# A hand-ordered kernel with one load queue, three row tiles loaded ahead of the first weights, and norms on GpSimd

## The chip, the core and the metric

The kernel runs on one core of one Trainium2 chip. A core has five engines that run on their own: TensorE (PE in the profile, with PEld for its weight loads), VectorE (DVE), ScalarE (ACT), GpSimd (POOL) and SyncE (SP), which here only issues transfers. DMAs are issued from SP's queue (q1 in the profile) and from ACT's queue (q10). The metric is the time of one execution in microseconds of device time, smaller is better; the median of three runs is given for the kernel before.

## What is computed

Two branches share one normalised input and are multiplied at the end:

```python
x  = A_q                                    # 1 x 2048 x 512, bfloat16
xn = layernorm(x)
# branch A: shift convolution, long convolution along the sequence, gate
k_shift = sum over t<4 of shift(A_k, 3 - t) * A_shift_k[:, 3 - t]
kv = k_shift * A_v
y  = irfft(rfft(pad(kv)) * rfft(pad(A_ssm_k)))[:2048]   # length 4096
s  = xn * (y + kv * A_ssm_D)
# branch B: gated feed-forward
h  = gelu(xn @ B_w_gate) * (xn @ B_w_up)    # 512 -> 1792
g  = silu(h @ B_w_down)                     # 1792 -> 512
out = x + s * g
```

The Fourier transforms are done as matrix products with tables of sines that the kernel builds itself.

## The kernel before

**Stages.** The 2048 rows are 16 row tiles of 128, in four quarters of four. The rows are taken so that partition p holds rows 16p to 16p+15. For each quarter, `ln` takes mean and variance of each row tile (`bn_stats`, `bn_aggr`, lines 875 and 876), the reciprocal root (for quarter 0 a square root on ACT, line 888, and a reciprocal on DVE, line 889; for the others a power on POOL, line 892), and writes the normalised tile XN (line 901 on ACT, line 902 on DVE or POOL). `xn_transpose` makes xnT, the transposed tile that PE needs: for quarter 0 four PE transposes per row tile (line 925) and evacuations from PSUM (the accumulator memory, 8 banks) by ACT or DVE; for the later quarters one transposing DMA on SP (line 914). `unit` multiplies one quarter's xnT with 128 columns of the gate and up weights (a product of four matrix products each, line 1200, recorded under the helper's line 649), takes the gelu on ACT (line 1220) and multiplies on DVE into HT (1226 and 1229). For the first two column groups of quarter 0 the work comes in sixteen half products, one row tile each, so that PE can begin before all four tiles are there. `down` multiplies HT with the down weights, in groups of 4, 5 and 5 column groups.

**The long convolution.** The filter A_ssm_k is loaded as four tiles h0 to h3 (Hn), transposed on DVE in 32 x 32 blocks (line 944, tasks 50 to 53, one per tile, about 2 us each), goes through a first transform on PE (`stage1` "H", line 984, eight tasks: 97, 92, 102, 117, 112, 107, 122, 87), is evacuated by ACT, stored to the scratch ZH through ACT's queue (tasks 91 to 126), read back (BH) and transformed again (line 1055, `psf`). The key side: `kshift` forms the four-tap shift convolution of a group of four row tiles on DVE (lines 1032 to 1038, about 1.2 us per instruction, eight per group) and the product with V (line 1040, giving KV0 to KV3, tasks 138, 146, 154, 162). `stage1` "K" (line 973) transforms KV on PE (u = 6 and 7, tasks 236, 237, 241, 242, read KV3), stores to ZK through SP, reads back (BK), transforms again (`psk`), multiplies spectra on DVE, transforms back (`inverse`, `psi`), stores to ZI and reads back (BI) for the last transform (line 1304).

**What sets the order.** Every instruction belongs to one of 802 numbered tasks. SEQ, a list written out in the program, gives the order in which tasks are emitted; a "b" behind a number takes the task's second engine. Each engine runs its own tasks in that order. `Trk` adds the semaphore waits from what tasks read and write, PSUM banks among them. `Sched.run` walks SEQ and gives each task a planned start and end from its costs; these plan times decide nothing at run time, except that a task which needs a bank or a buffer gets the one that is free first by the plan (`Pool_.find`). LAND holds the planned landing of each load; FIRST the time from which an engine is free in the plan; TAKEN a delay, per store that ACT issues early (`eng == "ACT"`), of the loads still under way.

**Loads.** ORDER gives the order in which loads are issued: x00, x01, x02 are row tiles 0, 1 and 2 with 3 (128, 128 and 256 KB); w0 to w3 are column groups of the gate and up weights (w0 two groups of 256 KB, the others 512 KB each); h0 to h3 the filter; k, v, d the keys, values and down weights. All are issued on SP, except w0, whose two loads are issued on ACT:

```python
"w": lambda i: load_w(i, ("ACT", "ACT") if i == 0 else ("SP", "SP"))
```

PE begins with 12 products without meaning (`warm_up`), which raise its clock before the first real product.

Of the kernel before, what the change touches and what calls it, by code (L numbers as in the profile page):

```python
# [22 lines left out]
LN_EPS = 1e-5  # L23
TURN = 8192
N_WARM = 12
ORDER = "x00 x01 w0 x02 w1 h0 h1 w2 h2 h3 D0 x1 s0 k0 w3 k1 d0 k2 d1 v0 v1 k3 v2 v3 x2 x3"
SEQ = (
# [23 lines left out]
)  # L51
NF_BANKS = 8
ISSUE = 470.0
LAND = {"x0_0": 3000, "x0_1": 4850, "wg0": 4500, "wu0": 6300, "x0_2": 6650, "wg1": 8150, "wu1": 9650, "h0": 11200, "h1": 12500, "wg2": 14000, "wu2": 15500, "h2": 16800, "h3": 18050, "D": 18500, "kz": 12600, "x1": 19350, "sk": 21850, "kh1": 23200, "kh113": 23400, "k0": 24700, "wg3": 26200, "wu3": 27700, "k1": 29000, "wd0": 31500, "k2": 32900, "wd1": 37000, "v0": 39000, "v1": 40400, "k3": 41700, "v2": 42950, "v3": 44250}
W_XT, W_SW, W_BK, W_BH, W_ZI, W_BI, W_ZK, W_MI, W_G1 = 850000, 690000, 685000, 688000, 310000, 575000, 600000, 329000, 150000
T_BH, T_BK, T_BI, T_X = 900.0, 500.0, 1500.0, 900.0
NC_PAIRS = 4
# [238 lines left out]
class Sched:  # L296
# [6 lines left out]
    OVL = {"DVE": 80.0, "ACT": 100.0}  # L303
    DMA_BW = 370.0
    SHARE_BW = 300.0
    FIRST = {"loads": 300.0, "SP": 37000.0, "ACT": 1600.0}
    DRAIN, DRAIN2 = 121.0, 97.0
    EARLY, LATE, SHARED, WAIT, TAKEN = 31000.0, 36500.0, 47000.0, 3300.0, 0.0

    def __init__(self):  # L310
        self.tasks = []
# [40 lines left out]
    def run(self):  # L352
        free = dict(self.FIRST)
        pipe = 0.0
# [66 lines left out]
def build_kernel(nc, A_q, A_k, A_v, A_shift_k, A_ssm_k, A_ssm_D, B_w_gate, B_w_up, B_w_down, out):  # L421
    with ExitStack() as es0:
# [104 lines left out]
        def dsem(name):  # L527
            return DSem(nc.alloc_semaphore(name), name)
# [92 lines left out]
        def dma(eng, out_ap, in_ap, sem, r, w):  # L621
            trk.dma(eng, lambda e: e.dma_start(out=out_ap, in_=in_ap), sem, r=r, w=w)  # L622
# [3 lines left out]
        def load(name, out_ap, in_ap, w_res, w_buf, nbytes, ring="SP", r=(), rb=()):  # L626
            sem = dsem("d_" + name)
            last_load[0] = S.add([("loads", ISSUE)], lambda e: dma(ring, out_ap, in_ap, sem, r, w_res), r=rb, w=w_buf, nbytes=nbytes, land=float(LAND[name]))

# [194 lines left out]
        def load_x0(t):  # L824
            ts = slice(*((0, 1), (1, 2), (2, 4))[t])
            load(f"x0_{t}", X[:, ts, :], x_dr[:, ts, :], R_X[ts], bX[0][ts], 131072 * (ts.stop - ts.start))

        def load_w(i, rings=("SP", "SP")):
            f0, n = FC[i]
            for nm, W, src, ring in (("g", Wg, wg_dr, rings[0]), ("u", Wu, wu_dr, rings[1])):  # L830
                load(f"w{nm}{i}", W[:, :, 128 * f0:128 * (f0 + n)], src[:, :, 128 * f0:128 * (f0 + n)], [R_Wc[nm, i]], [bW[nm][i]], 131072 * n, ring)

        def load_h(k, ring):
            load(f"h{k}", Hn[:, k, :], h_dr[:, k, :], [R_Hn[k]], [bHn[k]], 524288, ring)
# [27 lines left out]

        for what in ORDER.split():
            if what[0] == "x" and len(what) == 3:
                load_x0(int(what[2]))
                continue
            {"k": load_k, "v": load_v, "w": lambda i: load_w(i, ("ACT", "ACT") if i == 0 else ("SP", "SP")), "x": load_x, "d": load_wd, "h": lambda i: load_h(i, "SP"), "s": load_taps, "D": load_d}[what[0]](int(what[1:]))


        t_stats = [None] * NT  # L870
# [457 lines left out]
        for j in range(6):  # L1328
            d_out.append(dsem(f"d_out{j}"))
            g = G[:, 2 * j:2 * j + 2, :].rearrange("p t d -> p (t d)")  # L1330
            x = X[:, 2 * j:2 * j + 2, :].rearrange("p t d -> p (t d)")
# [17 lines left out]
def bass_recurrent_scan__ssm_conv_h3__glu_gated_geglu__prompt_kernel(  # L1349
    nc: bass.Bass,  # L1350
    A_q: bass.AP,
    A_k: bass.AP,
    A_v: bass.AP,
    A_shift_k: bass.AP,
    A_ssm_k: bass.AP,
    A_ssm_D: bass.AP,
    B_x: bass.AP,
    B_w_gate: bass.AP,
    B_w_up: bass.AP,
    B_w_down: bass.AP,  # L1360
    out: bass.AP,
):
    build_kernel(nc, A_q, A_k, A_v, A_shift_k, A_ssm_k, A_ssm_D, B_w_gate, B_w_up, B_w_down, out)
# [28 lines left out]
```

## Time and profile before

| | us |
|---|---|
| median of 3 runs (lowest, highest) | 186.76 (186.75, 187.11) |
| profiled execution, whole | 186.69 |
| its span, first to last instruction | 184.9 |
| PE busy / share of the span | 178.2 / 96% |
| DVE busy | 168.3 / 91% |
| ACT busy | 141.7 / 77% |
| POOL busy | 17.7 / 10% |
| mean granted clock of PE | 0.999 |

Times within the trace count from the first instruction of the span. A row of the timeline has start, length, engine (a q marks an issue by the engine's sequencer), line, operation, what it writes `<-` reads, shape, the number of instructions merged, and in brackets the idle time before it and what ended it. Matrix products overlap in PE, so that the length of one row reaches into the next: the pace is read from start to start. A row of waits has the total, the number of times, and the longest. A row of grouped instructions has busy time and mean ns, then the idle time before them. A DMA row ends with the median from issue to landing.

### The profile page before, as it was taken

How to read it: one execution, taken by the hardware profiler on the slowest of the kernel's cores; microseconds unless marked ns; L12 is line 12 of the kernel's file. 1: busy time of each engine (PE TensorE's matmuls, PEld its weight loads, DVE VectorE, ACT ScalarE, POOL GpSimd, SP SyncE). 2: the span in 40 equal slices, each digit the busy share in tenths (PEclk: the TensorE clock that was granted, in tenths of full speed). 3: DMA queues.
4: the chain of work that ended last, by engine and by line, in shares of the span. 5: the costliest groups of instructions: out<-in, count | busy, mean ns of one | idle time of the engine just before them, and what ended most of it. 6: DMA issues, size and time to landing. Idle time of an engine off the chain costs nothing.

```text
span 184.9 us, 3811 instructions
## 1 busy us (share of the span) xinstructions
PE 178.2 (96%) x1522; PEld 77.7 (42%) x1522; DVE 168.3 (91%) x250; ACT 141.7 (77%) x204; POOL 17.7 (10%) x29
## 2 busy tenths in 40 slices
PE   8599999979999999999999999999999999999993
PEld 3474444434443443433434433343333344445552
DVE  5998999999999999999579999999999997459994
ACT  3599798996489999998379798887898875238771
POOL 4000190890000000002200000000000000000000
PEclk9999999999999999999999999999999999999999
DMA  5999999999891959887999999688317154599338
GB/s 150 340 376 397 307 362 375 397 415 249 244 303 62 292 212 273 258 286 273 214 311 263 309 377 346 222 312 261 113 60 273 34 184 136 179 381 395 127 119 281
DMA packets 38683, 48.38 MB, mean 262 GB/s; under 512 B 9483, under 2 KB 28427, under 8 KB 38666
## 3 DMA queue, kind: packets, MB, share of 16 engines
q1 hardware_dynamic: 31082, 39.23, 67.7%
q10 hardware_dynamic: 7584, 8.91, 13.9%
q8 instruction: 12, 0.20, 0.4%
q14 instruction: 5, 0.04, 0.1%
HBM read 27.39 MB, written 14.68 MB: 228 GB/s over the span
## 4 chain that ended last, share of the span: by engine, by line
PE 85%; DMA 6%; DVE 4%; SPq 3%; issue 0%; ACT 0%
PE psall L649 67%; DMA Hn<-in_A_ssm_k_dram 6%; PE psall L1250 6%; PE psall L1055 6%; SPq L622 3%; PE psall L973 2%; DVE HTr L944 2%; PE psall L984 2%; PE psall L1304 2%; DVE HT L1226 0%; DVE HT L1229 0%; DVE G L1272 0%; DVE G L1271 0%; ACT G L1269 0%; DVE NB__68 L897 0%
## 5 line engine op out<-in xcount | busy, mean ns | idle before, releaser
L649 PE MATMUL psall<-xnT,Wg 128*128 128x512 bf16 (+1 forms) x248 | 55.6, 359 | 0.0
L649 PE MATMUL psall<-xnT,Wu 128*128 128x512 bf16 (+1 forms) x248 | 54.9, 359 | 0.1
L649 PE MATMUL psall<-Wd,HT 128*128 128x512 bf16 (+1 forms) x182 | 40.3, 368 | 1.0 <-DVE HT L1229 1.0
L1220 ACT ACTIVATE GE<-psall 128x512 bf16<-128x512 f32 x54 | 31.8, 608 | 9.4 <-PE psall L649 6.8
L649 PEld LDWEIGHTS psall<-xnT,Wu 128*128 128x128 bf16 x248 | 22.1, 98 | 26.3 <-issue 2.0
L649 PEld LDWEIGHTS psall<-xnT,Wg 128*128 128x128 bf16 x248 | 21.6, 98 | 26.5 <-issue 2.6
L1229 DVE TENSOR_TENSOR HT<-psall,GE 128x512 bf16<-128x512 f32 x36 | 24.1, 683 | 6.0 <-PE psall L649 5.8
L640 ACT ACTIVATE BO<-psall 128x1024 bf16<-128x1024 f32 x21 | 21.1, 1024 | 6.3 <-PE psall L1055 3.9
L649 PEld LDWEIGHTS psall<-Wd,HT 128*128 128x128 bf16 x182 | 16.2, 98 | 21.5 <-issue 2.6
L1158 DVE TENSOR_TENSOR HSW<-KB,HSW 128x2048 bf16<-128x2048 bf16 x16 | 19.1, 1218 | 0.1
L640 ACT ACTIVATE HSW<-psall 128x1024 bf16<-128x1024 f32 x14 | 13.9, 1023 | 5.4 <-PE psall L1055 5.3
L1038 DVE TENSOR_TENSOR KAC<-KAC,KTM 128x2048 bf16<-128x2048 bf16 x12 | 15.2, 1263 | 0.1
L1036 DVE TENSOR_TENSOR KTM<-KK,SKB 128x2048 bf16<-128x2048 bf16 x12 | 14.8, 1234 | 0.0
L640 ACT ACTIVATE KB<-psall 128x1024 bf16<-128x1024 f32 x14 | 13.8, 1029 | 1.3 <-PE psall L1055 1.2
L1250 PE MATMUL psall<-Wd,HT 128*64 128x512 bf16 (+1 forms) x112 | 12.7, 366 | 0.0
L1261 ACT ACTIVATE G<-psall 128x512 bf16<-128x512 f32 x12 | 6.9, 595 | 7.2 <-PE psall L649 7.1
L875 DVE BATCH_NORM_STATS2 stats<-X 128x6 f32<-128x512 bf16 x16 | 10.7, 682 | 1.1 <-DMA X<-in_A_q_dram 1.1
L640 ACT ACTIVATE U__73<-psall 128x512 bf16<-128x512 f32 x18 | 10.8, 637 | 0.1
L640 ACT ACTIVATE XN<-psall 128x1024 bf16<-128x1024 f32 x10 | 10.0, 1030 | 0.4 <-DMA ZH<-XN 0.4
L1263 DVE SCALAR_TENSOR_TENSOR G<-G,psall 128x512 bf16<-128x512 bf16 x12 | 7.9, 679 | 2.4 <-ACT G L1261 2.3
L1181 DVE TENSOR_TENSOR HSW<-HSW 128x2048 bf16<-128x2048 bf16 x8 | 9.6, 1216 | 0.0
L1158 DVE TENSOR_TENSOR KB<-KB,HSW 128x2048 bf16<-128x2048 bf16 x8 | 9.6, 1218 | 0.0
(94 smaller groups left out, 182.6 us busy)
## 6 DMA issues: line engine op xcount, KB each, us to landing
BH<-ZH SPq DMA_DIRECT2D x8, 512.0 KB, 5.4
HSW<-HSW SPq DMA_DIRECT2D x16, 256.0 KB, 2.9
BK<-ZK SPq DMA_DIRECT2D x8, 512.0 KB, 5.8
ZI<-BO ACTq DMA_DIRECT2D x16, 256.0 KB, 2.3
BI<-ZI SPq DMA_DIRECT2D x8, 512.0 KB, 6.7
ZH<-XN ACTq DMA_DIRECT2D x5, 512.0 KB, 3.4
ZK<-AST SPq DMA_DIRECT2D x5, 512.0 KB, 2.8
Hn<-in_A_ssm_k_dram SPq DMA_DIRECT2D x4, 512.0 KB, 9.2
```

Source lines behind the costliest of these rows:

```text
L640: return h.activation(o, i, ACTF.Copy, scale=scale)
L649: return h.matmul(o, lhsT=l, rhs=r, start=st, stop=sp)
L875: t_stats[t] = op([("DVE", 670.0)], lambda e, h, t=t: h.bn_stats(stats[:, t, :], X[:, t, :]), r=[bX[q][t % 4]], w=[bst[t]], rr=[R_X[t]], w ...
L1036: op([("DVE", dur)], lambda e, h, j=j, m=m: h.tensor_tensor(KTM[:, m.slot, :, :], kk(j), sk(j), ALU.mult), r=need + [bSKB[j], a], w=[m], r ...
L1038: op([("DVE", dur)], lambda e, h, m=m: h.tensor_tensor(KAC[:, a.slot, :, :], KAC[:, a.slot, :, :], KTM[:, m.slot, :, :], ALU.add), r=[m], ...
L1055: trk.op("PE", lambda h: h.matmul(ps(s, i)[b, :], lhsT=wt(col)[a, :], rhs=data(col)[a, :], start=n < 16, stop=n >= len(todo) - 16, tile_po ...
L1158: return hd.tensor_tensor(pair(KB, *(2 * DM * z for z in slots())) if to else x, k, x, ALU.mult)
L1181: return hd.tensor_tensor(x, x, y, ALU.add)
L1220: gelu_set.append(op([("ACT", act(512))], lambda e, h: h.activation(GE[:, g.slot, :], bank(pg), ACTF.Gelu_apprx_tanh), r=[pg], w=[g], rr=l ...
L1229: op([("DVE", dve(512, 1))], lambda e, h: h.tensor_tensor(HT[:, q % 2, m, :], bank(pu), GE[:, g.slot, :], ALU.mult), r=[pu, g], w=[bHT[q][m]],
L1250: trk.op("PE", lambda h, m=m, i=i, c=c: h.matmul(pc()[c, :], lhsT=HT[:, q % 2, m, 128 * jt + 64 * i:128 * jt + 64 * i + 64], rhs=Wd[:, m, ...
L1263: op([("DVE", dve(512, 1))], lambda e, h, g=g, pc=pc: h.scalar_tensor_tensor(out=g, in0=g, scalar=1.0, in1=pc(), op0=ALU.add, op1=ALU.mult ...
```

## The change

Four things change in the text. The two loads of w0 are issued on SP like the rest, and ORDER puts x02 ahead of w0. LAND gets new values. The plan's TAKEN becomes 1450 and ACT is free at 800 in place of 1600. SEQ is a new order of the same 802 tasks, with another choice of engine for nineteen of them. The choice of POOL for the norms of quarter 0 was there before (line 903) and is now taken for row tiles 0 to 2.

```diff
-ORDER = "x00 x01 w0 x02 w1 h0 h1 w2 h2 h3 D0 x1 s0 k0 w3 k1 d0 k2 d1 v0 v1 k3 v2 v3 x2 x3"
+ORDER = "x00 x01 x02 w0 w1 h0 h1 w2 h2 h3 D0 x1 s0 k0 w3 k1 d0 k2 d1 v0 v1 k3 v2 v3 x2 x3"
 SEQ = (
-    "0 17 18 ... 47 2 9 3 4 10 6 8 7 5 55 56 63 1 11 57 64 58 66 "
-    "65 67 77 127 78 68 79 59 80 352 81 364 350 60 61 69 362 70 82 62 71 72 73 365 75 74 353 83 363 84b 366 351 354 85 86b 367 12 370 358 368 359 "
+    "0 17 18 ... 47 2 9 4 55 5 56 3 57 8 63 64 65b 58 66 1 6 67 "
+    "59 77 78b 79 68b 60 80 61 69 70 71b 10 127 62 362 350 81 82 72 364 73 352 351 365 83 353 363 74 85 84b 368 358 356 86b 75 354 357 369 370 "
...
-LAND = {"x0_0": 3000, "x0_1": 4850, "wg0": 4500, "wu0": 6300, "x0_2": 6650, "wg1": 8150, ... "wd0": 31500, "k2": 32900, "wd1": 37000, "v0": 39000, ... "v3": 44250}
+LAND = {"x0_0": 3100, "x0_1": 3560, "wg0": 6050, "wu0": 6850, "x0_2": 5060, "wg1": 8550, ... "wd0": 31300, "k2": 32600, "wd1": 34900, "v0": 36200, ... "v3": 41400}
...
-    FIRST = {"loads": 300.0, "SP": 37000.0, "ACT": 1600.0}
+    FIRST = {"loads": 300.0, "SP": 37000.0, "ACT": 800.0}
...
-    EARLY, LATE, SHARED, WAIT, TAKEN = 31000.0, 36500.0, 47000.0, 3300.0, 0.0
+    EARLY, LATE, SHARED, WAIT, TAKEN = 31000.0, 36500.0, 47000.0, 3300.0, 1450.0
...
-            ... "w": lambda i: load_w(i, ("ACT", "ACT") if i == 0 else ("SP", "SP")), ...
+            ... "w": lambda i: load_w(i), ...
```

The order that this gives to each engine, at the places that matter below (numbers are tasks, names are what they write):

| engine | before | after |
|---|---|---|
| DVE, start | 9, 10, 6, 7 (tables), 55 and 56 (statistics and aggregate of tile 0), 11, 57, 64 (reciprocal 0), 58, 65 (norm 0), 67, 68 (norm 1), 59, 60, 61, 70, 62, 71 (norm 2), 73, 74 (norm 3), 84, 86 (evacuations), 367, 355, 50, 51 (HTr0, HTr1), 373, 385, 389, 52, 53 (HTr2, HTr3), 361 | 9, 55, 56, 57, 64, 58, 6, 67, 59, 78 (evacuation), 60, 61, 70, 10, 62, 73, 74 (norm 3), 84, 86, 11, 355, 7, 367, 373, 50, 51, 389, 385, 361, 52, 53 |
| POOL, start | 2, 3, 4, 5 (tables, constants) | 2, 4, 5, 3, then 65, 68, 71 (norms 0, 1, 2) |
| POOL, from 22 us | 127, 15, 129, 14, 130, 128 (tap copies and table products), 455 (power), 16, 54 (the fold of D into HTr, line 951), 76 | 127, 15, 128, 130, 54 (fold), 129, 14, 455, 16, 76 |
| PE, start | two transposed tiles, half products, with the other two transposes among them; 14 half products before the first full unit, 11 full units before task 97 | the same, all 16 half products before the first full unit, 12 full units before task 97 |
| DVE, near 37 us | ... 416, 135, 456, 412, 421, 425 (last HT of quarter 0) | ... 421, 105, 416, 456, 412, 425, 135 |
| DVE, last tasks up to 162 (KV3) | among them 650, 651 (statistics of tile 15) | 646 (statistics of tile 13); 650, 651 behind 162 |
| PE, near 80 us | 532, 172, 236, 533, 534, 241, 237, 242 | the same |
| ACT, near 27 us | 101 (store of ZH2) behind 94; 96 behind 415 | 96 and 101 behind 419 |
| ACT, near 84 us | 243, 244 (K evacuations), 657 (XN14), 168, 535 (tanh) | 243, 535, 244, 655 (XN12), 168 |
| DVE, near 84 us | 652 (variance), 552, 556, 239, 557, 654 (bias), 655, 656, 658 (norms) | 652, 239, 654, 656, 657, 658 |

The nineteen tasks with another engine: norms 65, 68, 71 from DVE to POOL; evacuations 78, 178, 198, 275 and 739 and norms 564 and 657 from ACT to DVE; 169, 179, 274, 294, 301, 346, 733 and norms 565 and 655 from DVE to ACT.

More of the change, by code (lines that the diff above doesn't have):

```diff
@@ L53 @@
 ISSUE = 470.0
-LAND = {"x0_0": 3000, "x0_1": 4850, "wg0": 4500, "wu0": 6300, "x0_2": 6650, "wg1": 8150, "wu1": 9650, "h0": 11200, "h1": 12500, "wg2": 14000, "wu2": 15500, "h2": 16800, "h3": 18050, "D": 18500, "kz": 12600, "x1": 19350, "sk": 21850, "kh1": 23200, "kh113": 23400, "k0": 24700, "wg3": 26200, "wu3": 27700, "k1": 29000, "wd0": 31500, "k2": 32900, "wd1": 37000, "v0": 39000, "v1": 40400, "k3": 41700, "v2": 42950, "v3": 44250}
+LAND = {"x0_0": 3100, "x0_1": 3560, "wg0": 6050, "wu0": 6850, "x0_2": 5060, "wg1": 8550, "wu1": 10030, "h0": 11330, "h1": 12600, "wg2": 14100, "wu2": 15600, "h2": 16900, "h3": 18150, "D": 18600, "kz": 12600, "x1": 19500, "sk": 21850, "kh1": 23200, "kh113": 23400, "k0": 24700, "wg3": 26200, "wu3": 27700, "k1": 29000, "wd0": 31300, "k2": 32600, "wd1": 34900, "v0": 36200, "v1": 37500, "k3": 38800, "v2": 40100, "v3": 41400}
 W_XT, W_SW, W_BK, W_BH, W_ZI, W_BI, W_ZK, W_MI, W_G1 = 850000, 690000, 685000, 688000, 310000, 575000, 600000, 329000, 150000
@@ L866, in build_kernel @@
                 continue
-            {"k": load_k, "v": load_v, "w": lambda i: load_w(i, ("ACT", "ACT") if i == 0 else ("SP", "SP")), "x": load_x, "d": load_wd, "h": lambda i: load_h(i, "SP"), "s": load_taps, "D": load_d}[what[0]](int(what[1:]))
+            {"k": load_k, "v": load_v, "w": lambda i: load_w(i), "x": load_x, "d": load_wd, "h": lambda i: load_h(i, "SP"), "s": load_taps, "D": load_d}[what[0]](int(what[1:]))
         t_stats = [None] * NT
```

44 rows, old and new, of the table SEQ are left out of this document.

## The prediction

> **What bounds the kernel now.** I read the page's busy shares first, then what PE waited for, then busy time by stretch, then the timeline of DVE where PE was not full. The sum below is made against the profiled execution: 186.69 us, of which 184.9 are span and 1.79 lie around it; the median of the three runs is 186.76, 0.07 more.
>
> ```profile
> PE 178.2 (96%) x1522; PEld 77.7 (42%) x1522; DVE 168.3 (91%) x250; ACT 141.7 (77%) x204; POOL 17.7 (10%) x29
> PE psall L925 <- DVE XN L902: 1.7, 2, 1.5
> PE psall L649 <- DVE HT L1229: 1.0, 1, 1.0
> PE psall L984 <- DVE HTr L944: 0.2, 1, 0.2
> 8.68:21.80 13.12, 12.95 (x100) 7.36 (x101) 11.99 (x16) 11.60 (x24) 0.00 (x0) 1.00 1.06 368
> 17.70:80.20 62.50, 61.34 (x411) 26.09 (x408) 62.40 (x82) 54.28 (x82) 13.57 (x13) 1.00 0.95 292
> 80.00:155.00 75.00, 75.00 (x803) 29.59 (x802) 70.22 (x95) 60.05 (x77) 2.05 (x2) 1.00 0.75 234
> 155.00:181.20 26.20, 26.20 (x229) 12.96 (x198) 20.29 (x34) 14.63 (x20) 0.00 (x0) 1.00 0.66 234
> ```
>
> In the stretches the columns after the length are PE, PEld, DVE, ACT, POOL, granted clock, DMA. PE is full from 8.68 to 181.20 but for 0.2 us near 21.7 and about 1 us near 38; at 1.00 of its clock there is no other slack to win. What can be won is the front (products before 8.68 are thin) and those two waits. The second reading matters more: DVE is busy 62.40 of the 62.50 us from 17.70 to 80.20. Where DVE starts and where it ends:
>
> ```profile
> 5.84 11.83 DMA Hn<-in_A_ssm_k_dram
> 17.70 3.96 DVE L944 STREAM_TRANSPOSE HTr<-Hn 128x1024 int32<-128x1024 int32 x2 [0.61 <-DMA Hn<-in_A_ssm_k_dram]
> 78.96 1.21 DVE L1040 TENSOR_TENSOR V<-KAC,V 128x2048 bf16<-128x2048 bf16 x1
> 80.45 0.39 PE L973 MATMUL psall<-V,FT 64*128 64x512 bf16 x2
> ```
>
> The third long-filter load (h2) lands at 5.84 + 11.83 = 17.67, DVE begins its transpose at 17.70 and never rests until the last shifted product KV3 (task 162) ends at 78.96 + 1.21 = 80.17. PE's task 236 needs KV3 and starts at 80.45. So PE may come at most 0.28 us earlier there unless DVE does. Before 80 us the kernel has two bounds within 0.3 us of each other, and a change that speeds PE alone is stopped at task 236.
>
> **The change, part by part.**
>
> *First weights from ACT's queue to SP's.* Two issues leave ACT (which delayed its table load) and stand behind the three X loads on SP.
>
> ```profile
> X<-in_A_q_dram SPq DMA_DIRECT2D x2, 128.0 KB, 3.6
> Wg<-in_B_w_gate_dram ACTq DMA_DIRECT2D x1, 256.0 KB, 4.0
> Wu<-in_B_w_up_dram ACTq DMA_DIRECT2D x1, 256.0 KB, 4.9
> 3.99 0.69 DVE L875 BATCH_NORM_STATS2 stats<-X 128x6 f32<-128x512 bf16 x1 [1.10 <-DMA X<-in_A_q_dram]
> 5.84 4.03 SPq L622 DMA_DIRECT2D Hn<-in_A_ssm_k_dram  x2
> out_dram<-G SPq DMA_DIRECT2D x3, 128.0 KB, 2.2
> ```
>
> The X loads are issued first on SP now too, so their issue does not move; they only stop sharing the DMA engines. The first row tile is in use at 3.99; bounds for its landing L: 3.97 (nothing won) and 0.7 + 2.2 = 2.9 (the quickest 128 KB transfer here). I take 3.6. Later loads are issued about 1 us later on SP, but SP already sits in one issue for microseconds (h2 and h3 take 4.03 for two), so their order of bytes, not their issue, sets the landing: the same bytes stand ahead of h2, and I leave 17.67 as it is, plus or minus 0.2.
>
> *Norms of row tiles 0 to 2 to GpSimd, evacuation 78 from ACT to DVE.* POOL has no such row. Bounds from its rows of the same width:
>
> ```profile
> 22.54 0.64 POOL L1013 COPY SKB<-SKR 128x512 bf16<-128x512 bf16 x1 [19.79 <-DMA SKR<-in_A_shift_k_dram]
> 23.15 1.24 POOL L755 TENSOR_TENSOR TM<-TAB 128x512 f32<-128x512 f32 x1
> 5.19 0.69 DVE L875 BATCH_NORM_STATS2 stats<-X 128x6 f32<-128x512 bf16 x1
> 5.79 0.14 DVE L889 RECIPROCAL mv<-mv 128x1 f32<-128x1 f32 x1
> 6.01 0.38 DVE L902 TENSOR_SCALAR XN<-X,mv 128x512 bf16<-128x512 bf16 x1
> 6.45 0.40 PE L925 MATMUL psall<-ident,XN 128*128 128x128 bf16 x4 [1.45 <-DVE XN L902]
> 11.30 1.25 PE L649 MATMUL psall<-xnT,Wg 128*128 128x128 bf16 x8
> 18.88 1.89 PE L649 MATMUL psall<-xnT,Wu 128*128 128x512 bf16 x8
> 20.61 1.03 PE L649 MATMUL psall<-xnT,Wg 128*128 128x512 bf16 x4
> ```
>
> One norm costs 0.64 to 1.24 there against 0.38 on DVE; I take 0.8, nearer the copy, as it also has one tensor input. The first norm starts at about L + 1.65 (statistics, their aggregate, the second tile's statistics, reciprocal, at the spacing of the rows above: 0.73 + 0.10 + 0.60 + 0.22), so its transpose can start at 3.6 + 1.65 + 0.8 + 0.05 = 6.1 in place of 6.45, the second 0.8 later. On DVE the second tile's small steps and task 6 reach to L + 2.2, then come statistics (0.6), evacuation 78 (0.4 with its wait), an aggregate (0.1) and the fourth statistics (0.6): the third reciprocal near L + 3.9, the third norm on POOL until L + 4.9, the fourth on DVE until L + 5.5. The third tile is transposed and evacuated near L + 5.95; eight half products of a quarter unit each (0.22, from the unit below) and 0.2 of waiting for the fourth end the front at L + 7.95 = 11.55. Now the x8 row at 11.30 begins with four short ones (0.22), so the first full unit starts at 11.52 with two half products (0.45) still owed: 11.97. Won: 0.4 us, with bounds +1.0 (L 2.9, norm 0.64) and -1.4 (L 3.97, each norm 1.24 plus a hold-up of 0.45).
>
> *That hold-up,* seen where POOL and DVE both read two tensors:
>
> ```profile
> 31.73 1.21 DVE L1038 TENSOR_TENSOR KAC<-KAC,KTM 128x2048 bf16<-128x2048 bf16 x1
> 35.27 1.68 DVE L1038 TENSOR_TENSOR KAC<-KAC,KTM 128x2048 bf16<-128x2048 bf16 x1
> 35.84 1.41 POOL L951 TENSOR_TENSOR HTr<-HTr,Dt 128x128 bf16<-128x128 bf16 x1
> ```
>
> The same addition takes 1.21 alone and 1.68 beside POOL's fold. The Trainium skill, "SBUF — State Buffer", section "Who interferes with whom", says that a DVE instruction with two SBUF inputs or in a two-port mode and a GpSimd instruction share a port pair, and that the later one blocks for the whole instruction. That speaks against the norms on GpSimd; the 0.47 us row agrees in kind. By the page the fourth norm and the phase product (task 6) on DVE would each block POOL or be blocked once; by the rows alone I charge nothing in the middle value and 0.45 a norm at the bad end.
>
> *New order, PE.* PE now does twelve full units ahead of the first filter product (task 97), one more than before. A unit is (20.61 - 18.88) / 2 = 0.865 us, so task 97 comes at 11.55 + 12 x 0.865 = 21.93 instead of 21.80 with one unit more behind it: PE is 0.73 ahead and the 0.2 wait for the DVE transposes is gone. Near 38 us the last half-multiply that frees a bank (task 425) now stands ahead of one 1.2 us addition (135), and PE has one product more to do before it, so the 1 us wait goes too. PE alone would be 1.5 to 1.7 us ahead at 40 us, less 0.2 for one more switch to the split tiles of L973 (seven groups before task 241 ends instead of six).
>
> *New order, DVE.* Between h2's transpose and KV3 the order drops task 361 (0.3 us: from 21.57 to 21.86), 650 and 651 (statistics and aggregate, 0.6 and 0.1) and takes in 646 (statistics, 0.6).
>
> ```profile
> 21.57 0.40 DVE L1214 TENSOR_TENSOR HT<-psall,GE 128x256 bf16<-128x256 f32 x1
> 21.86 0.70 DVE L875 BATCH_NORM_STATS2 stats<-X 128x6 f32<-128x512 bf16 x1
> 11.63 3.95 DVE L944 STREAM_TRANSPOSE HTr<-Hn 128x1024 int32<-128x1024 int32 x2
> 84.16 1.21 DVE L643 CAST AST<-psall 128x1024 bf16<-128x1024 f32 x1
> ```
>
> Net 0.3 + 0.6 + 0.1 - 0.6 = 0.4 us less. Task 361 fits into the 0.61 us in which DVE waits for h2: with the front as above the first pair of transposes starts near 12.1, ends near 16.0 (3.95), and two multiplies at 0.6 and task 361 follow, until 17.5. So KV3 ends near 79.8, task 236 starts there at the earliest, and of PE's 1.5 us only 80.45 - 79.83 = 0.6 is kept. What comes next keeps it: the transposed XN of the third quarter,
>
> ```profile
> 83.51 1.18 SPq L622 DMA_DIRECT2D HSW<-HSW  x2
> 85.81 0.46 SPq L622 DMA_DIRECT2D ZK<-ASX  x1
> 86.62 3.94 SPq L914 DMA_TRANSPOSE xnT<-XN  x1
> xnT<-XN SPq DMA_TRANSPOSE x1, 7.2
> 93.98 1.89 PE L649 MATMUL psall<-xnT,Wg 128*128 128x512 bf16 x8
> ```
>
> lands at 86.62 + 7.2 = 93.8, 0.15 us before PE uses it. It runs behind the swaps and the last K stores, which all follow from tasks 172 to 242 and move with them; a tanh now stands between the last two K evacuations on ACT (0.5 us), but the bias step on DVE no longer waits behind three other tasks, and the store's issue stays ahead of its turn on the DMA. After 94 us both orders hold the same PE work and the same number of switches; the inverse products stand up to 2.8 us earlier, and DVE has 3.5 to 4 us less before the last of them: net two evacuations like the CAST row (2 x 1.21) move to ACT, which is 60.05 of 75 us busy, and a product or two at 0.6 move behind it. The tail has the same steps. The plan's new costs (LAND, TAKEN, FIRST) emit nothing; they only change which bank or buffer a task gets.
>
> *Sum:* -0.6 us, 186.69 - 0.6 = 186.1.
>
> **The rivals.**
>
> *The whole PE saving arrives.* It needs KV3 0.6 to 0.9 us earlier still.
>
> ```profile
> L1038 DVE TENSOR_TENSOR KAC<-KAC,KTM 128x2048 bf16<-128x2048 bf16 x3 | 4.2, 1405 | 0.0
> ```
>
> For it: between 26 and 42 us three such additions take 1405 ns in the mean against 1.21 us, 0.6 us in all, and the fold that stretches one now stands elsewhere. Against it: as many POOL instructions fall into the stretch as before. Then 186.69 - 1.5 + 0.2, about 185.4.
>
> *Nothing measurable.* The X tiles land no earlier (they were first on SP already), or h2 lands 0.2 to 0.4 later; HTr2 starts late by that much and KV3's 0.4 is spent. 186.5 to 186.9, say 186.7.
>
> *Slower.* GpSimd's three norms in a row push the front past the gap before h2's transpose. With L = 3.97 and 1.69 a norm (1.24 + 0.45) the third norm ends at 3.97 + 1.65 + 5.1 = 10.7, the half products near 13.4, the first transposes start near 13.9 and HTr2 at 13.9 + 3.9 + 1.5 = 19.3 instead of 17.70: KV3 1.2 late, PE 0.9 late at task 236: 187.6. It decides once the norms are so slow that HTr2 starts more than 0.7 us late. The copy's 0.64 speaks against it, the 1.24 row for it.
>
> **How the numbers follow.** Chances: DVE-bound forecast 0.45 (its own range 185.8 to 186.4), whole saving 0.14, nothing 0.20, slower 0.21. A measurement of this kernel tells about 0.2%, 0.37 us, from no change, so below 186.39 is faster. Six sevenths of the forecast and all of the first rival lie there: 0.38 + 0.14 = 0.52; same 0.07 + 0.20 = 0.27; slower 0.21. The range runs from 185.2 to 187.4, which leaves part of the first rival and the worst of the last out.
>
> **What would show it.** Right: transposes L925 from about 6.1, no PE wait for HTr or for HT L1229 near 38, DVE again without idle time from 17.7 to its fourth L1040, and a PE wait of half a microsecond or more for that one before an L973. Wrong: if PE has no wait there and is over 1 us ahead at 94 us, DVE was not the bound; if DVE's second pair of L944 starts after 18.0, or the POOL norms are over 1 us, the front was mis-sized; if PE waits after 94 us, the loss is in the new order behind it.

## The result and the profile after

The changed kernel takes 193.40 us in the median (192.17 to 193.85) against 186.87 for the kernel before on the same chip: 1.034 times as long, 95% interval 1.029 to 1.039. The forecast of 186.1 has the wrong sign, and the top of its range, 187.4, is 6 us short. The profiled execution took 193.85 us, 192.1 of them span; its last matrix products start at 188.20, against 181.03 before. Here and below, medians are over all executions, while ratios leave out those more than 1.5% above the fastest of the same kernel.

From the page, the busy shares and the granted clock of PE in 40 slices of 4.8 us:

```profile
PE 180.4 (94%) x1512; PEld 80.0 (42%) x1522; DVE 163.7 (85%) x245; ACT 142.4 (74%) x206; POOL 22.1 (12%) x32
...
PEclk9759999999999999999999999999999999999999
```

DVE has 4.6 us less to do than before, about as forecast, and that bought nothing. The clock, 0.999 in the mean before, drops in the second and third slices: it is at 0.50 from 7.3 to 14.1 us. Next the waits (total, number of times, longest):

```profile
PE psall L925 <- POOL XN L902: 3.5, 2, 1.9
...
ACT ASX L640 <- DMA ZK<-ASX: 2.4, 1, 2.4
...
DVE HT L1226 <- ACT U__73 L640: 2.1, 1, 2.1
...
PE psall L973 <- ACT ASX L640: 2.1, 1, 2.1
```

PE waits twice for a norm on GpSimd, and once for an evacuation (ASX, a buffer of the key side's first transform) that itself waits until a store has emptied its buffer; DVE waits behind the same evacuation. The timeline shows that they lie 70 us apart:

```profile
2.96 0.69 DVE L875 BATCH_NORM_STATS2 stats<-X 128x6 f32<-128x512 bf16 x1 [1.12 <-DMA X<-in_A_q_dram]
...
4.62 6.36 POOL L902 TENSOR_SCALAR XN<-X,mv 128x512 bf16<-128x512 bf16 x3 [1.85 <-DVE mv L889]
...
6.91 0.40 PE L925 MATMUL psall<-ident,XN 128*128 128x128 bf16 x4 [1.87 <-POOL XN L902]
...
15.66 1.89 PE L649 MATMUL psall<-xnT,Wg 128*128 128x512 bf16 x8
...
21.66 3.99 DVE L944 STREAM_TRANSPOSE HTr<-Hn 128x1024 int32<-128x1024 int32 x2
...
79.78 0.39 PE L973 MATMUL psall<-V,FT 64*128 64x512 bf16 x2 [2.06 <-ACT ASX L640]
...
84.50 1.22 DVE L1040 TENSOR_TENSOR V<-KAC,V 128x2048 bf16<-128x2048 bf16 x1
```

The first tile is in use at 2.96 instead of 3.99: the loads did what was hoped. Then three norms take 6.36 us. DVE's second pair of filter transposes, HTr2, starts at 21.66 and not at 17.70, 3.96 us late; KV3 starts at 84.50 and not at 78.96, 5.54 us late. The other 1.6 us go to the second place. Its cause stands in SP's issues, first of the kernel before:

```profile
46.12 1.22 SPq L1066 DMA_TRANSPOSE G<-FT  x1
49.93 1.45 SPq L1066 DMA_TRANSPOSE MI<-TFA  x1
...
67.75 0.47 SPq L622 DMA_DIRECT2D ZK<-ASX  x1
```

and then of the changed kernel:

```profile
68.78 1.64 SPq L1066 DMA_TRANSPOSE G<-FT  x1
73.20 1.21 SPq L1066 DMA_TRANSPOSE MI<-TFA  x1
74.45 0.58 SPq L622 DMA_DIRECT2D ZK<-ASX  x1
```

with this among SP's own waits:

```profile
SPq L1066 <- DMA G<-FT: 2.8, 1, 2.8
```

Two transposing loads (tasks 163 and 164, line 1066) stood in an empty stretch of SP and now stand ahead of the third ZK store. Both use one semaphore, so that the second is issued only when the first has landed; SP rests 2.8 us, and the store behind it goes out at 74.45. That move is in the new order and in no step of the prediction.

### The profile page after: what moved, and what is told of

Read it like the earlier page. It is cut to its first block, busy times and chain, and to the rows that moved or that the text cites. A ratio compares the mean times of both kernels' runs of the same rounds, so it can differ in the third digit from the quotient of the medians.

```text
span 192.1 us, 3801 instructions
## 1 busy us (share of the span) xinstructions
PE 180.4 (94%) x1512; PEld 80.0 (42%) x1522; DVE 163.7 (85%) x245; ACT 142.4 (74%) x206; POOL 22.1 (12%) x32
## 4 chain that ended last, share of the span: by engine, by line
PE 60%; DVE 26%; DMA 7%; POOL 2%; ACT 2%; issue 1%; DVEq 0%
PE psall L649 46%; DVE KTM L1036 6%; PE psall L1250 6%; DVE KAC L1038 5%; PE psall L1055 5%; DMA ZI<-BO 4%; DVE KAC L1032 2%; POOL XN L902 2%; DMA ZK<-ASX 2%; DVE HT L1226 2%; PE psall L1304 2%; DVE V L1040 2%; DVE stats L875 2%; DVE HT L1229 2%; DVE X L992 1%
## 5 line engine op out<-in xcount | busy, mean ns | idle before, releaser
L649 PE MATMUL psall<-xnT,Wg 128*128 128x512 bf16 (+1 forms) x248 | 56.7, 367 | 0.1
L649 PE MATMUL psall<-xnT,Wu 128*128 128x512 bf16 (+1 forms) x248 | 56.5, 365 | 0.2
L649 PE MATMUL psall<-Wd,HT 128*128 128x512 bf16 (+1 forms) x172 | 38.2, 366 | 1.0 <-issue 0.6
L649 PEld LDWEIGHTS psall<-xnT,Wg 128*128 128x128 bf16 x248 | 22.6, 102 | 26.9 <-issue 3.3
L640 ACT ACTIVATE BO<-psall 128x1024 bf16<-128x1024 f32 x23 | 23.2, 1025 | 9.3 <-PE psall L1055 3.5
L1158 DVE TENSOR_TENSOR HSW<-KB,HSW 128x2048 bf16<-128x2048 bf16 x16 | 19.3, 1220 | 0.2 <-ACT KB L640 0.2
L640 ACT ACTIVATE KB<-psall 128x1024 bf16<-128x1024 f32 x15 | 14.8, 1036 | 0.9 <-PE psall L1055 0.9
L1250 PE MATMUL psall<-Wd,HT 128*64 128x512 bf16 (+1 forms) x112 | 12.3, 366 | 0.0
L640 ACT ACTIVATE AST<-psall 128x1024 bf16<-128x1024 f32 x11 | 11.5, 1059 | 0.0
L892 POOL TENSOR_TENSOR mv<-mv,NHALF 128x4 f32<-128x4 f32 x3 | 4.1, 1352 | 59.9 <-DVE mv L886 59.9
L640 ACT ACTIVATE X<-psall 128x1024 bf16<-128x1024 f32 x8 | 8.2, 1030 | 2.5 <-PE psall L649 1.2
L1226 DVE TENSOR_TENSOR HT<-U__73,GE 128x512 bf16<-128x512 bf16 x18 | 7.9, 444 | 2.1 <-ACT U__73 L640 2.1
```

Of the source, the lines that this page charges most:

```text
L640: return h.activation(o, i, ACTF.Copy, scale=scale)
L649: return h.matmul(o, lhsT=l, rhs=r, start=st, stop=sp)
L1158: return hd.tensor_tensor(pair(KB, *(2 * DM * z for z in slots())) if to else x, k, x, ALU.mult)
L1226: op([("DVE", dve(512, 2))], lambda e, h: h.tensor_tensor(HT[:, q % 2, m, :], U_[:, ub.slot, :], GE[:, g.slot, :], ALU.mult), r=[ub, g], w ...
L1250: trk.op("PE", lambda h, m=m, i=i, c=c: h.matmul(pc()[c, :], lhsT=HT[:, q % 2, m, 128 * jt + 64 * i:128 * jt + 64 * i + 64], rhs=Wd[:, m, ...
```

## The experiments

The short names are those under which the expectations went on record. No experiment leaves out work; e3 adds products without meaning that later ones overwrite, and p1 adds operations whose results nobody reads. Starts are read from the profiled executions; the last two columns are the median and the ratio to the kernel before on the same chip with its 95% interval.

| kernel | HTr2 | KV3 | last PE row | median us | ratio |
|---|---|---|---|---|---|
| before | 17.70 | 78.96 | 181.03 | 186.87 | 1 |
| after | 21.66 | 84.50 | 188.20 | 193.40 | 1.034 (1.029 to 1.039) |
| e1 after, norms on DVE | 18.16 | 82.13 | 187.36 | 192.55 | 1.026 (1.019 to 1.034) |
| e2 before, norms on GpSimd | 21.02 | 82.58 | 184.57 | 190.30 | 1.019 (1.015 to 1.023) |
| e3 after, PE's pauses filled | 19.72 | 83.69 | 187.43 | 193.21 | 1.030 (1.022 to 1.037) |
| e4 before, loads alone | 16.95 | 79.42 | 181.40 | 186.91 | 1.000 (0.998 to 1.001) |
| e5 after, 163 and 164 early | 20.77 | 81.35 | 184.37 | 189.83 | 1.016 (1.012 to 1.019) |
| e6 e1 and e5 together | 17.87 | 79.28 | 182.81 | 188.49 | 1.007 (1.004 to 1.010) |
| e7 before, 163 and 164 late | 17.48 | 83.32 | 185.71 | 191.36 | 1.021 (1.016 to 1.025) |
| e8 e6, second half of before | 17.79 | 79.32 | 181.49 | 187.56 | 1.003 (1.000 to 1.007) |
| v1 e4, two table products early | 17.46 | 78.84 | 180.82 | 187.10 | 1.000 (0.998 to 1.002) |
| v2 e4, all table work early | 17.45 | 79.16 | 181.34 | 186.36 | 0.997 (0.995 to 0.999) |
| v3 v2, down weights early | 17.16 | 77.13 | 179.28 | 185.83 | 0.995 (0.993 to 0.997) |

**e1, the norms back on DVE.** The plan stays, so that banks and buffers are the same:

```diff
-            t.emit(t.eng)
+            t.emit("DVE" if t.n in (65, 68, 71) else t.eng)
```

> The changed kernel with the plan as it is (so the same banks and buffers), only that the norms of row tiles 0 to 2 are done by DVE at their places in the order and not by GpSimd. Theory A, the three norms at 2.1 us are the cause of the late front, and the wait of 2.4 us near 77 follows from it: the second pair of L944 starts at 18.0 to 18.3 (h2 lands at 18.02) and not at 21.66, no wait of ACT for ZK<-ASX, time 186 to 187. Theory B, the front is due to the norms but the wait near 77 is of the new order itself: the front as in A, the wait stays at 2 us or more, time 188.5 to 190. Rival C, the loads or the lower granted clock make the front late, whichever engine norms: L944 still past 20, time over 191.

Theory B, and worse: the front is repaired (first full unit at 11.56, HTr2 at 18.16), but the wait at SP stays, and the median falls by 0.85 us only, with intervals of the two ratios that overlap. In the timeline of PE,

```profile
77.40 0.39 PE L973 MATMUL psall<-V,FT 64*128 64x512 bf16 x2 [1.63 <-ACT ASX L640]
```

and in busy time by stretch (PE, PEld, DVE, ACT, POOL, granted clock, DMA) the pause has a sequel:

```profile
78.00:81.00 3.00, 3.00 (x8) 1.06 (x7) 2.15 (x4) 3.00 (x6) 0.00 (x0) 0.50 0.51 200
81.00:82.00 1.00, 1.00 (x5) 0.39 (x4) 1.00 (x2) 1.00 (x3) 0.00 (x0) 0.78 0.00 0
```

After the pause PE ran at half its clock for some 3.4 us. One execution of this kernel with a mean clock of 1.00 took 190.42; the other three, at 0.99, took 192.04 to 194.07.

**e2, the norms on GpSimd in the kernel before.** The same line, with "POOL" in the kernel before; task 127, which waits for the taps, goes behind 71.

> The kernel before, with loads and order as they were; only norms 65, 68 and 71 go to GpSimd (and GpSimd's copy 127, which waits for the taps, stands behind the third of them). If one norm is 2.1 us there whatever surrounds it: three ends at about 8.2, 10.3 and 12.4, the half products end 2.5 to 4 us later than in the kernel before, granted clock below 1.00 in that stretch, time 189.5 to 192. If the 2.1 us came from what surrounds it in the changed kernel (statistics on DVE beside it), norms near 0.8 and time 186.5 to 187.5.

```profile
5.94 4.14 POOL L902 TENSOR_SCALAR XN<-X,mv 128x512 bf16<-128x512 bf16 x2 [3.19 <-DVE mv L889]
11.43 2.07 POOL L902 TENSOR_SCALAR XN<-X,mv 128x512 bf16<-128x512 bf16 x1 [1.35 <-DVE mv L876]
```

A norm takes 2.07 us here too, so it isn't the surroundings. HTr2 starts 3.32 us late, KV3 3.62, the last PE row 3.54: what DVE loses ahead of HTr2 arrives at the end whole, as a bound without slack should show. PE's clock is at 0.50 from 9.6 to 13.0 us here too, but full again when the third norm ends at 13.50.

**p1, what makes a GpSimd operation slow.** Eight operations on 128x512 in GpSimd's idle time:

```diff
+            for f in (lambda h: h.tensor_copy(y, x),
+                      lambda h: h.tensor_scalar(y, x, 1.0, None, ALU.mult),
+                      lambda h: h.tensor_scalar(y, x, 1.0, 1.0, ALU.subtract, ALU.mult),
+                      lambda h: h.tensor_scalar(y, x, a, None, ALU.mult),
+                      lambda h: h.tensor_scalar(y, x, a, b, ALU.subtract, ALU.mult),
...
+                      lambda h: h.tensor_tensor(y, x, x, ALU.mult)):
```

> The kernel before, with eight operations on 128x512 bfloat16 added to GpSimd's idle time after 2.8 us, each on data that nobody reads: copy, multiply by a constant, subtract and multiply by constants, multiply by a value per partition, subtract and multiply by values per partition (twice, as the norm does it, and once with 128x256), product of two tensors. If GpSimd's TENSOR_SCALAR goes by elements at 4.1 to 4.4 ns each, whatever its operands (as 128x128 in 0.56 us): each 128x512 TENSOR_SCALAR 1.9 to 2.3 us, the 128x256 one 1.0 to 1.15, the copy 0.64. If the values per partition make it slow: 0.7 to 1.0 with constants and 2.1 with values. If the second operation does: one-operation forms near 1.0. Whole time 186.5 to 187.5, as nothing waits for it.

GpSimd's timeline, in the order of the list:

```profile
3.39 0.61 POOL L699 COPY XN<-XN 128x512 bf16<-128x512 bf16 x1
4.09 1.50 POOL L700 TENSOR_SCALAR XN<-XN 128x512 bf16<-128x512 bf16 x1
5.67 1.93 POOL L701 TENSOR_SCALAR XN<-XN 128x512 bf16<-128x512 bf16 x1
7.71 1.69 POOL L702 TENSOR_SCALAR XN<-XN,mv 128x512 bf16<-128x512 bf16 x1
9.50 2.08 POOL L703 TENSOR_SCALAR XN<-XN,mv 128x512 bf16<-128x512 bf16 x1
...
15.16 1.04 POOL L706 TENSOR_TENSOR XN<-XN 128x512 bf16<-128x512 bf16 x1
```

The operation sets the price: 1.50 for one constant, 0.4 more for a second operation, 0.15 to 0.19 more for values per partition, against 0.61 for a copy. The 128x256 norm took 1.22, and the kernel 186.99 us in its one execution. None of the three theories came out as stated: one price per element misses the 1.50 and 1.69, and values per partition and a second operation each add less than was expected of them. The form counts for more than the number of inputs: the product of two tensors is done in half the norm's time. The Trainium skill, "GPSIMD Engine Reference", section "4. When to use GPSIMD", calls an elementwise operation with one input on this engine roughly line-rate. For the copy that is near (0.61 us; DVE's copy of that size out of PSUM took 0.42 in e1); for the norm it isn't, 2.08 us against 0.41 on DVE in e1, and the measurement decides.

**e3, PE's pauses filled.** Five, four and two products without meaning ahead of the transposes of tiles 0, 1 and 2:

```diff
+                        for _ in range((5, 4, 2, 0)[j] if k0 == 0 else 0):
+                            trk.op("PE", lambda h, p=p: mm(h, bank(p), ONE[:, 0:128], ONE, True, True), w=R_bank(p), accum=True)
```

> The changed kernel, with 5, 4 and 2 products without meaning ahead of the transposes of row tiles 0, 1 and 2, so that PE does not rest while GpSimd norms (about 0.36 us each at full clock). The norms stay at 2.1 us. If half of the late front is the lower granted clock that PE gets after the pauses: granted clock 1.00 through the front, first full unit at 13.2 to 14.2 in place of 15.66, time 190.5 to 192.3. If the clock costs nothing because GpSimd's third norm sets the end anyway: first full unit later than 15.2, time 193 to 194.

Busy time by stretch, with the clock third from the end, of the changed kernel and then of e3:

```profile
8.00:10.00 2.00, 1.02 (x10) 1.03 (x11) 0.56 (x4) 0.59 (x3) 2.00 (x2) 0.50 1.06 401
10.00:12.00 2.00, 2.00 (x22) 2.00 (x20) 0.81 (x2) 1.97 (x5) 0.98 (x1) 0.50 1.04 394
```

```profile
8.00:10.00 2.00, 1.21 (x20) 1.04 (x20) 0.55 (x4) 0.72 (x3) 2.00 (x2) 1.00 1.08 387
10.00:12.00 2.00, 2.00 (x33) 1.60 (x31) 1.34 (x3) 1.97 (x5) 0.96 (x1) 1.00 1.03 399
```

Half the late front was the clock: with the same norms the first full unit starts at 13.73 and HTr2 at 19.72, 1.93 and 1.94 us earlier than in the changed kernel. The Trainium skill, "TensorE: Matmul & The Clock Gate", "Part 1: The HAM clock gate (the "warmup" mystery)", says that PE falls to half its clock after an idle window of some 3.4 us. Here it fell at 7.3 us, after one pause of 1.87 us and four transposes; the second pause, of 1.67 us, came at half clock already. So a shorter pause was enough here. But the median is 193.21, no gain that can be told, and that part of the expectation (190.5 to 192.3) was missed. Of the 1.94 us won at HTr2, 1.27 are left at KV0 (45.80 against 47.07), for PE and DVE wait for each other and for ACT near 29 and 36 us, and 0.81 at KV3, as PE's pause at SP's store is 2.40 us long instead of 2.06.

**e5, the two transposing loads early again.** In the changed order, 163 and 164 behind 165:

```diff
-... 151 528 165 487 ... 224 472 163 164 154 ...
+... 151 528 165 163 164 487 ... 224 472 154 ...
```

> The changed kernel, with one thing moved on SP: the two transposing loads G<-FT and MI<-TFA (tasks 163 and 164) stand behind MI<-TFB near 47 us again and not ahead of the third ZK store near 69. GpSimd still norms. Theory A, the pause near 77 comes from SP's order (MI<-TFA may only be issued when G<-FT has landed, and ZK<-ASX stands behind it): ZK<-ASX issued within 1 us of its evacuation, no wait of ACT for ZK<-ASX, KV3 2 to 2.5 us earlier than 84.5, time 190 to 191.5. Rival, the pause comes from the late front (the keys' chain and the stores meet at a bad moment): it stays, 193 to 194.

The store goes out when its evacuation is done, and neither ACT nor PE waits for it:

```profile
71.21 0.36 SPq L622 DMA_DIRECT2D ZK<-ASX  x1
```

The median falls by 3.6 us, to 189.83, a little more than expected; in the profiled execution HTr2 too starts 0.89 us earlier (20.77), as the clock in front is at 0.50 for 3.4 us (8.8 to 12.3) and not for 6.8. The edit stands far behind the front, so that this part is taken for chance and not for the move's. KV3 is 3.15 us earlier, 2.26 of them gained behind HTr2.

**e6, both repairs.**

> Norms of row tiles 0 to 2 on DVE and the two transposing loads early: the rest of the change as it is. Theory A, these two are all that is wrong with the change, and the forecast of 186.1 would have held without them: 185.5 to 187. Rival, the rest of the new order costs too (in the kernel with norms on DVE alone PE lost about 1.5 us more after 95, at a wait of ACT for ZI<-BO at 135): 187.5 to 189.5, with waits after 95 us.

188.49: the rival is right. The two repairs bring 3.4% down to 0.7%; the rest of the change is still slower than the kernel before. Where, the waits of PE in e6 show:

```profile
PE psall L649 <- ACT X L640: 1.2, 1, 1.2
PE psall L1055 <- ACT BO L640: 1.1, 1, 1.1
```

the first at 34, the second at 131 us. Ahead of the first, ACT issues two stores, ZH<-XN, in one go and evacuates X only behind them:

```profile
31.22 1.83 ACTq L622 DMA_DIRECT2D ZH<-XN  x2
33.10 1.02 ACT L640 ACTIVATE X<-psall 128x1024 bf16<-128x1024 f32 x1 [3.04 <-DVE KAC L1038]
```

In the kernel before the same two stores go out at 26.74 and 30.10 and take 0.37 us each. They are tasks 96 and 101, which the new order puts one behind the other. That this makes the wait is read from the trace and was not tried.

**e7, the two loads late in the kernel before.** 163 and 164 behind 210, the second ZK store; nothing else.

> The kernel before with one thing moved on SP: G<-FT and MI<-TFA (tasks 163 and 164) from 46 us to between the second and the third ZK store, as in the changed kernel. Theory A: ZK<-ASX, issued at 67.75 before, goes at 72 to 74; ACT waits 2 to 5 us for it ahead of its next ASX evacuation (72.58 before), PE pauses as long, time 188.5 to 192. Rival, a late store is hidden: 186.5 to 187.3.

```profile
70.29 2.11 SPq L1066 DMA_TRANSPOSE MI<-TFA  x1
72.44 0.58 SPq L622 DMA_DIRECT2D ZK<-ASX  x1
```

```profile
ACT ASX L640 <- DMA ZK<-ASX: 3.3, 1, 3.3
...
PE psall L973 <- ACT ASX L640: 2.7, 1, 2.7
```

191.36, 2.1% slower: a move of two issues on SP, with every other engine's order unchanged, makes the wait in a kernel that didn't have it. KV3 is 4.36 us late. Here too the clock falls behind the pause, to 0.50 from 78.7 to 82.1 us; the one execution with a mean clock of 1.00 took 189.69, 1.4% over the kernel before, so that the store's wait by itself is worth less than 2.1%.

**e8, the later half of the old order.** e6 up to task 659 (about 87 us), then the tasks that are left in the order of before.

> The kernel with both repairs (norms on DVE, the two transposing loads early: 188.49) up to the transposing load of the third quarter's XN (task 659, about 87 us); every task behind it in the order and on the engines of the kernel before. Theory A, what is left of the loss (1.35 us) comes after 95 us, from the wait of ACT for ZI<-BO at 131 (1.1 us on PE) and from the last transform that ends 4.75 us ahead of the last product and not 3.88: both gone, 186.6 to 187.4, the ratio to the kernel before 0.997 to 1.002. Rival, the early order owes it all (PE waits of 0.27 and 1.23 us near 32 and 34): 188 to 189.

187.56, a little above the expected range. The wait at 131 is gone, and the last PE row starts at 181.49 instead of 182.81: of the 1.78 us by which e6's comes later than the old one, 1.32 came behind 87 us and 0.46 from the early part. Theory A holds for the larger part. This split is read from one execution of each; the intervals of the two ratios, 1.004 to 1.010 and 1.000 to 1.007, overlap.

**e4, the loads alone.**

```diff
-ORDER = "x00 x01 w0 x02 w1 ...
+ORDER = "x00 x01 x02 w0 w1 ...
-... load_w(i, ("ACT", "ACT") if i == 0 else ("SP", "SP")) ...
+... load_w(i) ...
```

> The kernel before with the loads alone changed: the first weights on SP's queue, behind the three X loads. Theory A, the loads are harmless: first statistics near 3.0 (3.99 before), h2 lands 0.2 to 0.4 later than 17.67, second pair of L944 no later than 18.1, time 186.4 to 187.2. Rival, the later loads (h2, keys, values) hold DVE up: 187.5 or more. Rival, the earlier X tiles pay: 186.2 or less.

No difference, though h2 landed at 16.93, earlier and not later. DVE was even 0.75 us ahead at HTr2, and lost it by KV0, where it was 0.46 us late (44.24 against 43.78). Two rows are long:

```profile
23.98 1.14 DVE L1226 TENSOR_TENSOR HT<-U__73,GE 128x512 bf16<-128x512 bf16 x1
...
25.64 1.53 DVE L992 TENSOR_TENSOR XN<-XN 128x1024 bf16<-128x1024 bf16 x1
```

**v1 and v2, GpSimd's table work out of DVE's way.** On top of e4; "b" here is GpSimd:

```diff
-... 15b ... 14b ... (v2 also: ... 16b ... 76b ...), 127 ahead of 15b
+... 15b 14b 127 ...             (v1)
+... 15b 14b 16b 76b 127 ...     (v2)
```

> The kernel before with the loads of the change, and on GpSimd the two table products (tasks 15 and 14, line 755) ahead of the four copies that wait for the taps, so that they run near 13 to 17 us and not from 23 to 27. In the run with the loads alone DVE began its second pair of L944 0.75 us earlier (16.95) and yet KV0 came 0.46 us later: L1226 took 1.14 us there and L992 1.53 (0.42 and 0.67 elsewhere), beside GpSimd's L755. Theory A, GpSimd's two-tensor products hold DVE up: with them elsewhere these two rows fall to 0.4 to 0.6 and 0.7, KV0 1 to 1.5 us earlier than 44.24, KV3 likewise, time 185.6 to 186.5. Rival, the rows are long for another reason: KV0 at 44.0 to 44.5, time 186.7 to 187.3.

> As the kernel with the table products early, and the rest of the table's work on GpSimd (their sum, line 758, and the turned copies, lines 642 and 643, tasks 16 and 76) early too, from about 16 to 22 us instead of 34 to 42. Theory A (GpSimd's long rows hold DVE's two-tensor rows up; DVE's 32-bit transposes and reads of PSUM beside them are not held up): L1038 near 35 falls from 1.69 to 1.21 and the three rows at 39 to 43 from 1.43, 1.32 and 1.23 to 1.21, KV3 another 0.6 to 0.9 us earlier, time 185 to 186.2, or no better than with the products alone where PE is the bound by then. Rival, DVE's transposes pay for it (3.95 a pair becomes 4.5 or more): 186.5 to 188.

In v1 the L992 row is short and L1226 down to 0.76; KV0 comes 0.58 us earlier than in e4, less than the 1 to 1.5 expected, and the time is that of before. In v2 the rows near 35 to 43 are all at 1.20 to 1.23, and KV0 starts 1.54 us earlier than in e4. DVE's transposes beside GpSimd's table work take 3.98 and 3.96 a pair (3.95 and 3.96 before). The time, 186.36, is just above the expected range and 0.3% below the kernel before. Of the lead at KV0 0.60 us is left at KV1 (59.94 against 60.54) and 0.26 at KV3, for PE now waits for a load:

```profile
40.87 3.41 PE L649 MATMUL psall<-Wd,HT 128*128 128x512 bf16 x15 [1.13 <-DMA Wd<-in_B_w_down_dram]
```

**v3, the down weights early.**

```diff
-... k1 d0 k2 d1 v0 v1 k3 v2 v3 ...
+... k1 d0 d1 v0 v1 k2 k3 v2 v3 ...
```

> As the kernel with all table work on GpSimd early (186.36), and the second down weights (wd1) and two value loads are issued ahead of the third key load. In that kernel DVE was 1.5 us earlier at KV0 (42.70), but PE then waited 1.13 us for wd1, which landed at 40.83, and DVE lost its lead waiting for PE. Theory A, the down weights are the next bound: they land near 39.3, no wait of PE for Wd, KV3 about 0.8 us earlier than 79.16, time 185.2 to 186.0. Rival, the transposed XN of the second quarter (landed at 51.78, used at 51.92) is the bound behind it, as all loads end near 47 anyway: PE waits there 0.5 us or more instead, time 186.1 to 186.7.

Theory A: 185.83, 0.5% faster than the kernel before (ratio 0.993 to 0.997), and so faster than both kernels. From v2 it can't be told: the intervals overlap. PE waits for no down weights; its only waits for loads are two of half a microsecond for Wu, at 7 and 16 us. The timeline of DVE, then busy time by stretch:

```profile
34.44 1.21 DVE L1038 TENSOR_TENSOR KAC<-KAC,KTM 128x2048 bf16<-128x2048 bf16 x1
...
41.95 1.22 DVE L1040 TENSOR_TENSOR V<-KAC,V 128x2048 bf16<-128x2048 bf16 x1
...
77.13 1.22 DVE L1040 TENSOR_TENSOR V<-KAC,V 128x2048 bf16<-128x2048 bf16 x1
```

```profile
17.70:80.20 62.50, 62.49 (x416) 26.66 (x415) 62.40 (x86) 55.34 (x84) 6.57 (x7) 1.00 0.95 299
```

KV3 starts 1.83 us earlier than before, and the last PE row 1.75, in a profiled execution that at 184.96 us is the fastest of its seven; by the medians on the same chip the gain is 1.2 us. PE and DVE are both full from 17.7 to 80.2: the two bounds of the prediction's first part, moved together.

## Why the prediction was wrong

**The norm on GpSimd was mis-sized.** The step "One norm costs 0.64 to 1.24 there against 0.38 on DVE; I take 0.8, nearer the copy, as it also has one tensor input" measured 2.1 us, above both bounds and above the 1.69 of the bad end. The rows were chosen by width and number of inputs. Two rows of the same operation stood in GpSimd's list of the kernel before:

```profile
2.19 0.56 POOL L695 TENSOR_SCALAR ident<-K 128x128 bf16<-128x128 int32 x1
...
38.02 0.94 POOL L642 TENSOR_SCALAR TFA<-TF 128x256 bf16<-128x256 bf16 x1
```

Scaled by width they give 4 x 0.56 = 2.2 and 2 x 0.94 = 1.9 us. With them the lower bound alone would have put HTr2 past the 0.7 us from which the "slower" rival was said to decide. Two of the prediction's own signs of this came: norms over 1 us, and a second pair of L944 that starts after 18.0.

**The rival had the mechanism, not the price.** Its chain ran from a third norm ending at 10.7 to HTr2 at 19.3. With the measured end, 4.62 + 6.36 = 10.98, it gives 19.58, and e3 has 19.72: right where the clock is kept up. The changed kernel has 21.66; the 1.9 us between them is the half clock after PE's pause, in no term of the sum. That KV3 and PE's end follow HTr2, as e2 shows, was right.

**A move on SP was left out.** The late stretch was argued with "the last K stores, which all follow from tasks 172 to 242 and move with them", and the end of KV3 was counted from DVE's own tasks. 163 and 164 had gone in front of the third ZK store, ahead of all these, and were in neither: the evacuation that this store holds up keeps DVE waiting 2.1 us in the changed kernel, before KV3. e7 prices them at 2.1% by themselves, and e5, without them, is 3.6 us faster than the changed kernel, some 0.9 of it from the clock in front. By itself this omission turns the forecast round.

**"After 94 us both orders hold the same PE work"** is true and didn't suffice: in the profiled executions the later half costs 1.3 us (e6 against e8), with a wait of PE for the evacuation of BO in it, and no wait behind 94 us was worked out. What holds that evacuation up in e6 isn't settled: the trace names a PE product there, and the store ZI<-BO in e1 (2.4 us) and in the changed kernel (1.4 us).

**DVE's 0.4 us less did not arrive.** In e6, without the other faults, KV3 ends at 79.28 + 1.22 = 80.50, not at 79.8, and DVE is busy 61.48 of the 62.50 us. One row, beside GpSimd's second table product, is 0.7 us long:

```profile
28.68 1.91 DVE L1036 TENSOR_TENSOR KTM<-KK,SKB 128x2048 bf16<-128x2048 bf16 x1
```

**What held.** The X tiles' landing came at the good bound (2.96, where 2.9 was given), and task 97 in e6 at 21.88 (21.93 forecast). The wait of 1 us near 38 went, but one of 1.23 came at 34.

**The hold-up was charged to the wrong place.** The norms on GpSimd were not lengthened by DVE (2.12 us in the mean, 2.08 in p1), while the fourth norm on DVE took 0.65 at 10.48 beside the third on GpSimd. And the addition of 1.68 us was read as held up by GpSimd's fold, which also carries the first rival ("the fold that stretches one now stands elsewhere"). But the fold began 0.57 us behind the addition (35.84 against 35.27); what was under way was the sum of the table products, line 758, first in the kernel before and then, beside the same addition, in v1:

```profile
34.48 1.39 POOL L758 TENSOR_TENSOR TF<-TM,TM 128x512 bf16<-128x512 f32 x1
```

```profile
35.26 2.01 POOL L758 TENSOR_TENSOR TF<-TM,TM 128x512 bf16<-128x512 f32 x1
34.91 1.21 DVE L1038 TENSOR_TENSOR KAC<-KAC,KTM 128x2048 bf16<-128x2048 bf16 x1
```

Where the sum begins first, the addition is long; where the addition begins first, the sum is long (2.01 against 1.28 in v2, where it runs beside transposes). In v3, with the sum gone, the addition takes 1.21 and the fold, begun 0.35 us behind it, 1.17 against 0.42 in e6. The Trainium skill's rule, "SBUF — State Buffer", section "Who interferes with whom", speaks of one port pair shared by DVE's two-input operations and GpSimd, where the later of two blocks, and these runs bear that out.

**The landing of h2** was given as 17.67 plus or minus 0.2; among kernels with the new loads it came from 16.93 (e4) to 18.13 (e1), so the margin was too small.

What stays open: when a pause halves the clock. In these traces it stays down for 3.41 us or twice that (7.29 to 14.11 in the changed kernel, 78.03 to 81.44 in e1, 78.73 to 82.14 in e7). In the 3.41 us ahead of the drops in e1 and e7 PE was busy for a share of 0.49 and 0.51. The changed kernel's pause of 2.06 us lies across a step of this kind, counted on from 14.11 to 78.96, with shares of 0.63 and 0.74 on its two sides, and the clock stayed at 1.00. But in e3 a stretch of that length with 0.46 left it at 1.00 too, so that PE's busy share alone doesn't decide. What the 1.23 us at 34 costs by itself wasn't tried either.

## What to carry to other kernels

Price a moved operation by rows of the same operation on the new engine, scaled by size, before rows of the same size with another operation. When an order changes, list each queue's issues before and after side by side, and for every issue that has moved name what stands behind it and which buffer that frees: here two issues on SP cost as much as three norms (1.021 and 1.019, each with a drop of the clock in it). A lead on one engine is kept only until its next shared resource: of the 1.54 us that v2 won at KV0 by moving GpSimd's work, 0.26 were left at KV3, and the next load was what PE then waited for. Moving that load without GpSimd's work wasn't tried.

## What was unexpected of the hardware

A subtract and multiply by values per partition on 128x512 took 2.08 us on GpSimd, 3.4 times the copy of the same size (0.61) and twice the product of two tensors (1.04). PE's clock fell to 0.50 for 3.4 us after one pause of 1.63 us in a stretch that was otherwise full (e1), and pauses up to 2.40 us left it at 1.00 in other runs. And the loss from GpSimd and DVE working side by side goes to whichever begins later: in e6 GpSimd's product, begun 0.29 us behind a product of DVE, took 2.02 us in place of 1.05, and DVE's next product, begun 1.20 us behind GpSimd's, took 1.91 us in place of 1.2.
